# DRAM copies of weight strips and residual tiles laid out in eight row groups with gaps

## The chip, the cores and the metric

The kernel runs on one core of one Trainium2 chip. The metric is the device time in microseconds (us) of one execution. The kernel before took 2142.14 us (median of 3 runs, 2141.03 to 2143.61).

Engine names in the profile: PE is TensorE's matrix multiplication, PEld its weight loads, DVE VectorE, ACT ScalarE, POOL GpSimd, SP SyncE, which issues nearly all DMA here (its queue q1 has 152,016 of the 158,307 packets). A trailing q (SPq) means the engine's sequencer. q1 is SyncE's DMA queue; q8 is a queue that fetches instructions.

## The reference

Four residual blocks in a row, layers A, B, A, B, on a sequence of 2048 rows of 576 values:

```python
x = x + _A_ref(_layernorm(x), A_wqkv, A_wo)
x = x + _B_ref(_layernorm(x), B_mem0, B_Wq, B_Wk, B_Wv, B_Wo, B_seg_len)
x = x + _A_ref(_layernorm(x), A_wqkv, A_wo)
x = x + _B_ref(_layernorm(x), B_mem0, B_Wq, B_Wk, B_Wv, B_Wo, B_seg_len)
```

`_A_ref` projects to q, k, v with a 576 x 1728 matrix, does a local attention over 8 positions with a step of 2, and projects back with a 576 x 576 matrix. `_B_ref` is an attention over 64 segments of 32 rows, one after the other, with 32 heads of 128 and a memory of 8 rows carried along. B's weights stay in SBUF. A's weights are not kept beside them: they lie in DRAM as twelve "strips" and are fetched again for each of the 32 tiles of 64 rows in both A layers.

## The kernel before

The DRAM copies, the ring of SBUF tiles that receives the strips, and the functions that fill them (cuts marked with `# ...`):

```python
dp = self.pool("dram", 1, space=bass.MemoryType.DRAM)
self.x1T = dp.tile([P, NT, 5, T], F32, name="x1T")           # residual tiles, P = 128
self.x3T = dp.tile([P, NT, 5, T], F32, name="x3T")
self.strips = [dp.tile([P, 5 * 256], BF16, name=f"strip{i}") for i in range(12)]
# ...
tiles("ring", 3, [P, 5 * 256])                               # three tiles in SBUF
# ...
def wload(self, i, src, rows, col0, n, prio, dep):
    # ...
    w = pl.buf("ring") if k else None
    # ...
    def fetch(e):
        dma(out=w.t[:, 0:5 * n], in_=self.strips[i][:, 0:5 * n])      # n = 256 or 128
    # ...
    o = pl.op("SP", 0.9 if k <= COPY else 0.5, gather if k <= COPY else fetch, prio,
              [dep, self.strip_in.get(i)], acq=[w], lat=4.0)
    if k == COPY:
        self.strip_in[i] = pl.op("SP", 0.5, lambda e: dma(out=self.strips[i][:, 0:5 * n], in_=w.t[:, 0:5 * n]), prio, [o], uses=[w])
    return view, (w,), o
```

The first three uses of a strip gather it from the input (`COPY` is 2), the third also stores it compactly; later uses call `fetch`. The kernel plans the order of all instructions itself before it emits them: `pl.op` takes an estimated duration, and `lat=4.0` tells the plan that a refill lands 4.0 us after its issue. The matmuls that use a strip:

```python
def mm(e, c=c, view=view, ps=ps, w0=w0):
    for kc in range(5):
        nc.tensor.matmul(ps.t[:, c * T:(c + 1) * T], lhsT=view()[:, kc, w0:w0 + P], rhs=xn.t[:, kc, :],
                         start=(kc == 0), stop=(kc == 4))
```

Three strips (two of 320 KB, one of 160 KB) serve one group of 25 such matmuls, and the ring has three tiles. So a tile can be refilled only when the matmuls of the group before have left it.

## Time and profile before

| what | value | how to read it |
|---|---|---|
| time | 2142.14 us | the profiled execution spans 2133.8 us |
| TensorE busy | 2017.4 us | 95% of the span, so 116 us idle in all |
| TensorE waiting for strips | 7.0 us | lines L570 (qkv) and L680 (projection) |
| TensorE waiting for instructions ("issue") | 32.6 us | 66 waits |
| mean granted clock of TensorE | 0.987 | 1 is full speed |

The lines behind these are in the prediction. For the strips, this line of the kernel before has the issues by SyncE, with shortest, median and longest duration in ns, and first and last start in us:

```profile
L507 SPq DMA_DIRECT2D ring<-strip x732: 319/382/2679, 134.7 to 2048.2; - x183
```

The 732 refills are 244 groups of three. SyncE needs 0.38 us to issue one.

### The profile page before, as it was taken

How to read it: one execution, taken by the hardware profiler on the slowest of the kernel's cores; microseconds unless marked ns; L12 is line 12 of the kernel's file. 1: busy time of each engine (PE TensorE's matmuls, PEld its weight loads, DVE VectorE, ACT ScalarE, POOL GpSimd, SP SyncE). 2: the span in 40 equal slices, each digit the busy share in tenths (PEclk: the TensorE clock that was granted, in tenths of full speed). 3: DMA queues.
4: the chain of work that ended last, by engine and by line, in shares of the span. 5: the costliest groups of instructions: out<-in, count | busy, mean ns of one | idle time of the engine just before them, and what ended most of it. 6: DMA issues, size and time to landing. Idle time of an engine off the chain costs nothing.

```text
span 2133.8 us, 132983 instructions
## 1 busy us (share of the span) xinstructions
PE 2017.4 (95%) x60717; PEld 1732.3 (81%) x60717; DVE 1416.8 (66%) x3754; ACT 1137.8 (53%) x2803; POOL 832.5 (39%) x1289
## 2 busy tenths in 40 slices
PE   1688999999999999999999999999999999999998
PEld 1577888888888888888888888888888888888876
DVE  4477676766666666766766676667667666665565
ACT  1354555555555555555555555555555555655554
POOL 3235434444343344434444443343444334342320
PEclk7899999999999999999999999999999999999999
DMA  9744343343443344334333433334344333331220
GB/s 324 201 148 141 122 127 123 124 138 106 126 127 121 113 124 141 113 117 127 126 116 117 142 121 119 116 127 127 118 128 130 115 117 124 123 121 59 75 76 10
DMA packets 158307, 265.14 MB, mean 124 GB/s; under 512 B 23464, under 2 KB 89904, under 8 KB 157616
## 3 DMA queue, kind: packets, MB, share of 16 engines
q1 hardware_dynamic: 152016, 237.38, 35.5%
q0 software_dynamic: 4576, 18.88, 2.6%
q8 instruction: 474, 7.77, 1.5%
q14 instruction: 89, 0.73, 0.1%
q10 hardware_dynamic: 1152, 0.39, 0.1%
HBM read 240.46 MB, written 16.12 MB: 120 GB/s over the span
## 4 chain that ended last, share of the span: by engine, by line
PE 89%; DMA 6%; issue 2%; DVE 2%; ACT 1%; SPq 0%; ACTq 0%; DVEq 0%
PE r L832 29%; PE r L994 18%; PE r L879 17%; PE r L570 7%; PE r L835 7%; DMA ring<-strip 3%; PE r L970 3%; PE r L680 2%; PE r L644 2%; PE r L470 2%; PE r L929 1%; PE r L919 1%; DMA x<-in_B_mem_dram 1%; PE r L619 1%; PE r L923 1%
## 5 line engine op out<-in xcount | busy, mean ns | idle before, releaser
L832 PE MATMUL r<-hT,wq 128*128 128x80 bf16 (+1 forms) x8832 | 660.3, 198 | 4.6 <-ACT hT L276 2.8
L832 PE MATMUL r<-hT,wk 128*128 128x80 bf16 (+1 forms) x8832 | 662.5, 199 | 1.5 <-issue 1.3
L832 PEld LDWEIGHTS <-wq 128*128 128x128 bf16 x8832 | 500.9, 99 | 47.7 <-issue 35.0
L835 PE MATMUL r<-hT,wqk_r 128*128 128x160 bf16 (+1 forms) x2208 | 507.1, 230 | 0.2 <-issue 0.2
L276 ACT ACTIVATE qk<-r 128x480 bf16<-128x480 f32 (+2 forms) x668 | 351.0, 526 | 265.7 <-PE r L835 254.7
L832 PEld LDWEIGHTS <-wk 128*128 128x128 bf16 x8832 | 447.1, 99 | 1.5 <-issue 1.4
L994 PE MATMUL r<-OT,wo 128*128 128x80 bf16 (+1 forms) x11040 | 418.6, 200 | 27.6 <-issue 22.9
L994 PEld LDWEIGHTS <-wo 128*128 128x128 bf16 x11040 | 394.8, 100 | 39.4 <-issue 34.5
L879 PE MATMUL r<-wv,hT 128*32 128x512 bf16 x5376 | 355.5, 381 | 2.4 <-issue 2.0
L283 POOL TENSOR_TENSOR big<-qT,kT 128x1024 bf16<-128x1024 bf16 x189 | 314.7, 1685 | 60.3 <-ACT kT L276 33.7
L283 POOL TENSOR_TENSOR ex<-ex,sum 128x320 bf16<-128x320 bf16 x138 | 106.9, 775 | 570.7 <-DVE sum L779 509.2
L879 PEld LDWEIGHTS <-hT 128*32 128x32 bf16 x6720 | 173.1, 96 | 127.8 <-issue 5.0
L276 ACT ACTIVATE V<-r 128x512 bf16<-128x512 f32 x305 | 181.4, 596 | 159.2 <-PE r L879 159.1
L835 PEld LDWEIGHTS <-wqk_r 128*128 128x128 bf16 x2208 | 219.7, 99 | 0.5 <-issue 0.4
L768 DVE TENSOR_REDUCE nmx<-r 128x8 f32<-128x320 f32 x276 | 133.3, 483 | 108.6 <-PE r L923 108.4
L276 ACT ACTIVATE OT<-r 128x320 bf16<-128x320 f32 (+1 forms) x378 | 134.4, 423 | 112.3 <-PE r L970 111.7
L570 PE MATMUL r<-xn,ring 128*128 128x64 bf16 x4725 | 176.9, 194 | 15.6 <-DMA ring<-in_A_wqkv_dram 11.6
L570 PEld LDWEIGHTS <-ring 128*128 128x128 bf16 x4725 | 157.4, 98 | 34.5 <-issue 14.1
L276 ACT ACTIVATE big<-r 128x256 bf16<-128x256 f32 (+1 forms) x288 | 109.1, 430 | 89.4 <-PE r L644 88.4
L283 POOL TENSOR_TENSOR xnb<-x,st 128x256 bf16<-128x256 f32 x124 | 64.6, 521 | 205.4 <-DVE st L476 205.4
L1013 DVE CAST hT<-r 128x64 bf16<-128x64 f32 (+1 forms) x68 | 14.9, 219 | 194.9 <-PE r L994 194.8
L769 DVE TENSOR_TENSOR r<-r,nmx 128x320 f32<-128x320 f32 x276 | 137.8, 499 | 9.5
(147 smaller groups left out, 2978.6 us busy)
## 6 DMA issues: line engine op xcount, KB each, us to landing
ring<-strip SPq DMA_DIRECT2D x488, 320.0 KB, 3.5
ring<-strip SPq DMA_DIRECT2D x244, 160.0 KB, 4.0
x1T<-x SPq DMA_DIRECT2D x32, 160.0 KB, 3.9
x<-x1T SPq DMA_DIRECT2D x32, 160.0 KB, 4.1
x3T<-x SPq DMA_DIRECT2D x32, 160.0 KB, 4.5
x<-x3T SPq DMA_DIRECT2D x32, 160.0 KB, 4.5
wo<-in_B_Wo_dram POOLq DMA_DIRECT2D x4, 1152.0 KB, 26.0
wq<-in_B_Wq_dram POOLq DMA_DIRECT2D x2, 2048.0 KB, 20.6
```

The lines of the kernel that those rows point to most:

```text
L276: nc.scalar.activation(out=out, in_=in_, func=ACT.Copy, scale=1.0 if scale is None else scale)
L283: (self.nc.vector if e == "DVE" else self.nc.gpsimd).tensor_tensor(out=out, in0=in0, in1=in1, op=op)
L470: nc.tensor.matmul(psf, lhsT=(self.ones if c < 4 else self.ones_h)[:, :], rhs=xs.t[:, c].rearrange("p a t -> p (a t)"), start=(c == 0), st ...
L570: nc.tensor.matmul(ps.t[:, c * T:(c + 1) * T], lhsT=view()[:, kc, w0:w0 + P], rhs=xn.t[:, kc, :], start=(kc == 0), stop=(kc == 4))
L644: nc.tensor.matmul(ps[g].t[:, c * P:(c + 1) * P], lhsT=self.epadT[q4, c0 + c, :], rhs=e_.t[q4].rearrange("p w t -> p (w t)"), start=True, ...
L768: nc.vector.tensor_reduce(out=m, in_=v, axis=AX.X, op=ALU.max, negate=True)
L769: nc.vector.tensor_tensor(out=v, in0=v, in1=m.unsqueeze(len(shp) - 1).to_broadcast(shp), op=ALU.add)
L832: nc.tensor.matmul(pv[:, hh, wi, a:b], lhsT=self.Wb[wi][0][:, kc, h * P:(h + 1) * P], rhs=hT.t[:, kc, a:b], start=(hh == 0 and wi == 0 and ...
L835: nc.tensor.matmul(pv[:, hh, :, a:b], lhsT=self.Wb[0][1][:, h * P:(h + 1) * P], rhs=hT.t[:, 4:6, a:b], start=False, stop=(hh == n - 1), sk ...
L879: nc.tensor.matmul(ps.t[c * 32:(c + 1) * 32, :], lhsT=l, rhs=w, start=(kc == 0), stop=(kc == 4))
L970: nc.tensor.matmul(ps[c].t[:, i * n + a - c0:i * n + z - c0], lhsT=V[b].t[q4, r, i, :], rhs=pt.t[q4, i, b, a:z], start=(i == 0 and b == bl ...
L994: nc.tensor.matmul(psY.t[:, mb * W80 + c0:mb * W80 + c1], lhsT=self.wo[:, w0:w0 + P], rhs=self.OT[:, h % 16 // 4 * 8 + h // 16 * 4 + h % 4 ...
```

## The change

Its intent, as far as the diff tells: to give the transfers of strips and residual tiles a slowest dimension of 8 on the DRAM side. A row group of 16 rows is followed by one unused row, so 8 x 16 rows can't be read as 128 rows with one stride.

```diff
+NQU = 8
+RQU = P // NQU
-        self.x1T = dp.tile([P, NT, 5, T], F32, name="x1T")
-        self.x3T = dp.tile([P, NT, 5, T], F32, name="x3T")
-        self.strips = [dp.tile([P, 5 * 256], BF16, name=f"strip{i}") for i in range(12)]
+        self.x1T = dp.tile([NQU, P // NQU + 1, NT, 5, T], F32, name="x1T")
+        self.x3T = dp.tile([NQU, P // NQU + 1, NT, 5, T], F32, name="x3T")
+        self.strips = [dp.tile([NQU, P // NQU + 1, 5 * 256], BF16, name=f"strip{i}") for i in range(12)]
@@ fetch
-            dma(out=w.t[:, 0:5 * n], in_=self.strips[i][:, 0:5 * n])
+            dma(out=w.t[:, 0:5 * n], in_=self.strips[i][:, 0:RQU, 0:5 * n])
@@ the strip's store, likewise [:, 0:RQU, 0:5 * n]; the residual tiles' store and load:
-  out=(self.x1T if layer == 1 else self.x3T)[:, j], in_=xT.t[:]
+  out=(self.x1T if layer == 1 else self.x3T)[:, 0:RQU, j], in_=xT.t[:]
-  out=b.t[:], in_=src[:, j]
+  out=b.t[:], in_=src[:, 0:RQU, j]
```

The two added lines of constants move the line numbers behind them by two: L570 before is L572 after. The plan is not told anything new, so the order of all instructions is the same.

More of the change, by code (lines that the diff above doesn't have):

```diff
@@ L512, in wload @@
         if k == COPY:
-            self.strip_in[i] = pl.op("SP", 0.5, lambda e: dma(out=self.strips[i][:, 0:5 * n], in_=w.t[:, 0:5 * n]), prio, [o], uses=[w])
+            self.strip_in[i] = pl.op("SP", 0.5, lambda e: dma(out=self.strips[i][:, 0:RQU, 0:5 * n], in_=w.t[:, 0:5 * n]), prio, [o], uses=[w])
         return view, (w,), o
@@ L688, in a_tile @@
                   pr(Q[6]), [o], uses=[ps, xT])
-        xst = pl.op("SP", 0.5, lambda e: nc.sync.dma_start(out=(self.x1T if layer == 1 else self.x3T)[:, j], in_=xT.t[:]),
+        xst = pl.op("SP", 0.5, lambda e: nc.sync.dma_start(out=(self.x1T if layer == 1 else self.x3T)[:, 0:RQU, j], in_=xT.t[:]),
                     pr(0.95), [o], uses=[xT])
@@ L714, in residual @@
         src = (self.x1T, self.x3T)[lane]
-        o = pl.op("SP", 0.5, lambda e: nc.sync.dma_start(out=b.t[:], in_=src[:, j]), prio,
+        o = pl.op("SP", 0.5, lambda e: nc.sync.dma_start(out=b.t[:], in_=src[:, 0:RQU, j]), prio,
                   [dep, (self.x1_stored, self.x3_stored)[lane][j]], acq=[b] if xb is None else [b, xb])
```

## The prediction

Two words of the text: k is the number of completion packets that a transfer leaves on q1. In the trace of the kernel before it is 8 for the one transfer with 8 rows and 16 for those with 128; I took it for the number of DMA engines that the transfer uses. A page is what one q8 packet carries: 16,384 bytes, 474 packets, about one per 256 instructions of TensorE. That k would fall to 8, and that the eight engines would be those of the 8-row load, was my assumption; the trace of the kernel before does not show it.

> **What bounds the kernel now.** I read the page first, then the waits of the matrix engine, the list of DMA issues and the records of single packets. From the page, in order: span, engines, DMA queues, the chain that ended last, DMA issues.
>
> ```profile
> span 2133.8 us, 132983 instructions
> PE 2017.4 (95%) x60717; PEld 1732.3 (81%) x60717; DVE 1416.8 (66%) x3754; ACT 1137.8 (53%) x2803; POOL 832.5 (39%) x1289
> ...
> q1 hardware_dynamic: 152016, 237.38, 35.5%
> ...
> q8 instruction: 474, 7.77, 1.5%
> ...
> PE 89%; DMA 6%; issue 2%; DVE 2%; ACT 1%; SPq 0%; ACTq 0%; DVEq 0%
> ...
> ring<-strip SPq DMA_DIRECT2D x488, 320.0 KB, 3.5
> ring<-strip SPq DMA_DIRECT2D x244, 160.0 KB, 4.0
> x1T<-x SPq DMA_DIRECT2D x32, 160.0 KB, 3.9
> ```
>
> TensorE is busy 95% of the span and 89% of the chain. SyncE's DMA queue (q1) takes 35.5% of sixteen engines; 732 of its transfers refill the three ring tiles with weight strips. q8 fetches instructions: 474 packets, one per 256 of TensorE's 121,500 instructions. The table of time stretches shows how full TensorE is between start and end (length, then busy time of PE, PEld, DVE, ACT, POOL, then granted clock, DMA share, GB/s):
>
> ```profile
> 300.00:700.00 400.00, 394.72 (x11759) 342.49 (x11755) 273.20 (x718) 222.02 (x538) 166.37 (x260) 1.00 0.39 122
> ```
>
> So a transfer matters only through TensorE's idle time. TensorE's waits (total us, times, longest):
>
> ```profile
> PE r L994 <- issue: 22.9, 34, 1.3
> ...
> PE r L680 <- DMA ring<-strip: 3.6, 9, 0.9
> PE r L570 <- DMA ring<-strip: 3.4, 6, 1.1
> ```
>
> Only 7.0 us go to late strips. The largest wait, "issue", is the instruction stream: of 66 issue waits of PE (32.6 us), 80% ended 1.25 to 1.53 us after a q8 packet had finished. All waits of PE sum to 36 us between 135 and 1900 us, so nothing can make this kernel 2% faster by waits of DMA alone.
>
> **How late a strip may be.** Each group of 25 matmuls (qkv part, or output projection) uses three strips: two of 320 KB, one of 160 KB. There are 244 such groups. SyncE issues a refill some 0.03 us after the first tile is free, the second 0.41 us and the third 0.90 us later (medians). From a strip's own issue to its first matmul, the third strip has 4.5 us at the tenth percentile, 4.9 at the quarter, 5.6 at the median; the second 4.7, 5.1, 5.9; the first 4.5 or more in 95%. The third lands 4.0 us after its issue (median). The room is thus small: about 1.6 us at the median, under 0.85 us in a quarter of the groups.
>
> [...] the one transfer with 8 rows (the load of the initial memory) left 8 data packets of 1152 bytes and 8 completion packets; the 128-row ones leave 16 completions. [...] q1's data packets in flight peak at 16, but at 15 while an instruction packet is in flight. [...] The trace has 474 packets of 16,384 bytes, mean 1.07 us each, and shows they are not wholly hidden (32.6 us above).
>
> **The change, part by part.** The programs hold the same instructions in the same order on all engines. What differs is 872 transfers: 732 refills, 12 strip stores, 128 stores and loads of residual tiles. Their DRAM side becomes 8 x 16 rows with a gap of one row, so it can't be merged to 128; SBUF's side stays 128. [...] Bytes and rows stay.
>
> *Packets.* Eight completions fewer per transfer: q1 should show 152,016 - 872 x 8 = 145,040.
>
> *Moving time.* A row of 2560 bytes takes an engine 102 ns (median), a row of 1280 bytes 55 ns. Eight rows per engine were 0.82 us (0.44 for the small strip); sixteen are 1.63 us (0.88). A set of three moves in 4.14 us instead of 2.07.
>
> *Landing.* I took 19 sets of three with no other SyncE transfer near, times from the first issue: first packet 0.96 us, last completion of the first strip 2.46, of the second 3.29, of the third 4.93 (medians), landing 0.4 after. The third varies from 3.7 to 5.3 us. With 0.42 us of moving after the second, 3.7 is what sixteen even engines give; the extra 1.2 us is about one 16 KiB packet, so I read it as one engine held up by an instruction fetch.
>
> *Which engine is that?* I followed each engine's packets (the next usually starts 3 to 4 ns before the last one ends) through the saturated start, from 26 us to the first instruction packet at 38.2 us. Its engine is not one of the eight that carried the 8-row load. If so, after the change the strips run on eight engines that TensorE's instruction packets do not use: half the engines, but no straggler, and an instruction fetch without strips in its way. This is the step I trust least; I give it 0.85.
>
> *Cost on the strips.* Strip 1 completes at 2.46 + 0.82 = 3.28, strip 2 at 3.28 + 1.63 = 4.91, strip 3 at 4.91 + 0.88 = 5.79 us after the first issue; plus 0.42 to land. From their own issues: 3.7, 4.9, 5.3 us, against 3.0, 4.05, 4.0 (medians) before. Set against the room in each of the 244 groups, and giving a third strip issued late credit for its lateness, 87 groups come short by 40 us together (mean 0.46). A wait inside a group helps the next one: its first tile is free and being refilled while TensorE still waits for the third. I take half off: 20 us, less the 7 us that exist: +13. The 7 us also contain straggler hits that vanish.
>
> *SyncE's issue.* An issue of the 128-row form takes 0.38 us, of the 64-row loads 0.48 (medians); I allow 0.1 us more per changed issue. The engines' queue is the limit then, so only the first strip sees it. About +4 us.
>
> *Instruction fetch.* From the point where TensorE passes half a page to the start of the fetch, 1.8 us pass when q1 is under 10% busy, and 2.6 when over 50%. Without strips there, I take half of 32.6 us off: -15. A matmul wait on a strip also gives a page time to come.
>
> *Other parts.* The 12 stores lie in the start, +2. Residual tiles (128 transfers) take about 0.5 us longer, off the path. Other engines' instruction packets may share the eight: +3.
>
> Sum: 13 + 4 - 15 + 2 + 3 = +7 on 2142; rounded up for what queues behind longer transfers: 2152.
>
> **Rivals.** *A: instruction packets share the eight engines.* For: I inferred the engine. Then the third strip is late by the full 2.07 us and the straggler stays; first-order shortfall with 0.9, 1.7 and 2.1 us added is 184 us in 157 groups, and page fetches wait longer. With relief and more "issue": 2290 to 2380. Against: the packet tracing. *B: everything hidden, or k stays 16.* For: only 7 us of strip waits now, DMA 39% busy. Against: a quarter of groups has under 0.85 us. It would make 2120 to 2145. *C: SyncE becomes the bound, if the new form is issued much slower.* 997 issues at 0.38 us are 380 us; even doubled they fit, but a third issue later than 1.5 us would add directly: 2180 to 2250. Against: the unmerged 64-row loads cost 0.48 us.
>
> **Range and chances.** The main case puts the time at 2120 to 2190; A (0.12) and C (0.08) reach far above. Range 2115 to 2250. Faster by over 2% needs 43 us, more than the issue waits hold: 0.04. Slower by over 2%: A and C, and a main case mis-sized in the relief: 0.25.
>
> **What would show it.** Right: 145,040 q1 packets; landing 4.3 us or so for 320 KB strips and 5.3 for 160 KB; waits of PE on strips 20 to 40 us in 60 to 100 waits; "issue" waits of PE halved; instruction packets near 0.9 us. Wrong: packets unchanged (k stayed 16); "issue" waits doubled, with instruction packets well over 1.07 us (A); SyncE issues near 1 us (C).

## The result

The changed kernel took 2311.47 us (median of 4 runs, 2308.09 to 2316.26), the kernel before in the same rounds 2141.59 us (4 runs, 2138.08 to 2143.61). The ratio is 1.0797, with a 95% interval of 1.0772 to 1.0821. Ratios here and below are the mean time of one kernel's runs over that of the other's of the same rounds, so not quite the ratio of the medians quoted. Executions over 1.5% slower than the fastest of the same kernel are left out of the means. The result is right in value (the output agrees with the reference). The predicted 2152 and its range up to 2250 were wrong.

The page of the changed kernel, in order: span, engines, the queues q1 and q8, and the chain that ended last, by engine and by line:

```profile
span 2306.4 us, 132983 instructions
...
PE 2068.6 (90%) x60717; PEld 1754.8 (76%) x60717; DVE 1421.1 (62%) x3754; ACT 1140.4 (49%) x2803; POOL 834.1 (36%) x1289
...
q1 hardware_dynamic: 145040, 237.35, 32.4%
...
q8 instruction: 474, 7.77, 1.4%
...
PE 59%; DMA 36%; issue 2%; DVE 1%; SPq 1%; ACT 0%; ACTq 0%; DVEq 0%
DMA ring<-strip 33%; PE r L834 19%; PE r L996 15%; PE r L881 7%; PE r L837 4%; PE r L572 4%; PE r L682 2%; PE r L972 2%; PE r L646 1%; DMA x<-in_B_mem_dram 1%; PE r L931 1%; PE r L472 1%; PE r L921 1%; DMA ring<-in_A_wqkv_dram 1%; PE r L621 1%
```

The instruction count is the same. q1 has exactly the predicted 145,040 packets: each changed transfer leaves eight completions instead of sixteen (872 x 8 = 6976 packets fewer), and I take it to go out on eight engines. The counts of packets in flight agree: after 300 us, with no instruction packet in flight, the commonest number of q1's data packets above zero is eight (36% of the time). In the kernel before it is sixteen (12%), and fifteen (8%) while an instruction packet is in flight. TensorE's share of the chain fell from 89% to 59%, and the refills now carry a third of it.

TensorE's waits (total us, times, longest us), with "issue" of the output projection for comparison:

```profile
PE r L572 <- DMA ring<-strip: 83.9, 158, 2.8
PE r L682 <- DMA ring<-strip: 31.2, 33, 1.8
PE r L996 <- issue: 21.8, 25, 3.1
```

Late strips cost 115.1 us in 191 waits instead of 7.0 in 15; 76 us of it, in 88 waits, stand before the eleventh matmul of a group, the first that uses the second wide strip. Over all lines, "issue" waits came to 41.6 us instead of 32.6 (here and below these are counted from 0.05 us up, strip waits from 0.15 us as in the lists of waits).

The span grew by 172.6 us. All waits of TensorE together went from 112.0 to 233.3 us (+121), and its busy time from 2017.4 to 2068.6 us (+51); the two sum to the whole. Of the +121, strips are 108 and issue 9. The +51 needs a closer look, because the work is the same. Two groups show most of it. The list of groups (count, busy us, mean ns of one, idle before), first of the kernel before:

```profile
L570 PE MATMUL r<-xn,ring 128*128 128x64 bf16 x4725 | 176.9, 194 | 15.6 <-DMA ring<-in_A_wqkv_dram 11.6 <-DMA ring<-strip 3.4 <-issue 0.2
L680 PE MATMUL r<-oT,ring 128*128 128x64 bf16 x1575 | 62.7, 193 | 3.9 <-DMA ring<-strip 3.6
```

and then of the changed one:

```profile
L572 PE MATMUL r<-xn,ring 128*128 128x64 bf16 x4725 | 207.9, 195 | 107.0 <-DMA ring<-strip 83.9 <-DMA ring<-in_A_wqkv_dram 14.2 <-issue 5.0
L682 PE MATMUL r<-oT,ring 128*128 128x64 bf16 x1575 | 66.8, 194 | 34.2 <-DMA ring<-strip 31.2 <-issue 3.0
```

One matmul takes the same 194 ns, yet the groups are busy 31.0 and 4.1 us longer. Matmuls overlap: 4725 of them at 194 ns would be 917 us, and 177 are counted. I read it so: a wait in the middle of a group breaks the overlap, and the last matmul before it is seen at full length. The 35 us over 176 additional waits are 0.2 us each, about the length of one matmul.

The rest fits the granted clock. The timeline of the changed kernel (start us, length us, engine, line, operation, count, and the wait in brackets) after one long wait:

```profile
1113.66 1.13 PE L572 MATMUL r<-xn,ring 128*128 128x64 bf16 x15 [2.47 <-DMA ring<-strip]
1114.60 0.46 PE L834 MATMUL r<-hT,wq 128*128 128x80 bf16 x4
1114.85 0.47 PE L834 MATMUL r<-hT,wk 128*128 128x80 bf16 x4
```

The same kernel in stretches of time (from:to, length, then busy time and count of PE, PEld, DVE, ACT, POOL, then granted clock, DMA share, GB/s):

```profile
300.00:700.00 400.00, 367.76 (x10770) 313.53 (x10767) 251.38 (x660) 204.51 (x495) 153.95 (x239) 1.00 0.35 113
1113.60:1116.80 3.20, 3.14 (x47) 3.02 (x48) 0.00 (x0) 0.44 (x1) 1.33 (x1) 0.52 0.36 113
1116.80:1120.00 3.20, 3.20 (x110) 2.11 (x107) 0.95 (x3) 1.60 (x3) 3.20 (x4) 1.00 0.35 126
```

After a wait of 2.47 us TensorE ran at half clock (0.5 in the clock records) until 1116.7. The counts, 47 matmuls in 3.2 us and 110 in the next, are partly of other kinds; but in the chain of this stretch eight matmuls of L834 take 0.53 us before 1116.7 and 0.29 after. The clock records hold 14 such periods (51.6 us) after the start phase, against 4 (13.8 us) in the kernel before; over the whole run the half-clock time was 109.7 us against 58.2. TensorE was busy in 72.1 us of it, against 23.4. The 48.7 us more of work at half speed are worth up to 24 us, if half clock doubles the time (the eight matmuls above took 1.8 times as long). With the 35 us above that is a little more than the 51 us, so the two overlap somewhere; their split is an estimate. The clock records of both kernels (12 before, 36 after) hold 0.5 and 1.0 only, and all but the last of each are 3.41 us long or a multiple of it.

### The profile page after: what moved, and what is told of

Same layout as the page of the kernel before. It is cut to its first block, busy times and chain, and to the rows that moved or that the text cites.

```text
span 2306.4 us, 132983 instructions
## 1 busy us (share of the span) xinstructions
PE 2068.6 (90%) x60717; PEld 1754.8 (76%) x60717; DVE 1421.1 (62%) x3754; ACT 1140.4 (49%) x2803; POOL 834.1 (36%) x1289
## 3 DMA queue, kind: packets, MB, share of 16 engines
q1 hardware_dynamic: 145040, 237.35, 32.4%
## 4 chain that ended last, share of the span: by engine, by line
PE 59%; DMA 36%; issue 2%; DVE 1%; SPq 1%; ACT 0%; ACTq 0%; DVEq 0%
DMA ring<-strip 33%; PE r L834 19%; PE r L996 15%; PE r L881 7%; PE r L837 4%; PE r L572 4%; PE r L682 2%; PE r L972 2%; PE r L646 1%; DMA x<-in_B_mem_dram 1%; PE r L931 1%; PE r L472 1%; PE r L921 1%; DMA ring<-in_A_wqkv_dram 1%; PE r L621 1%
## 5 line engine op out<-in xcount | busy, mean ns | idle before, releaser
L834 PE MATMUL r<-hT,wq 128*128 128x80 bf16 (+1 forms) x8832 | 664.4, 199 | 6.2 <-issue 2.9
L834 PE MATMUL r<-hT,wk 128*128 128x80 bf16 (+1 forms) x8832 | 665.6, 199 | 1.9 <-issue 1.9
L834 PEld LDWEIGHTS <-wq 128*128 128x128 bf16 x8832 | 504.5, 99 | 49.4 <-issue 36.9
L834 PEld LDWEIGHTS <-wk 128*128 128x128 bf16 x8832 | 449.8, 100 | 3.4 <-issue 3.3
L881 PE MATMUL r<-wv,hT 128*32 128x512 bf16 x5376 | 360.4, 385 | 1.5 <-issue 1.2
L572 PE MATMUL r<-xn,ring 128*128 128x64 bf16 x4725 | 207.9, 195 | 107.0 <-DMA ring<-strip 83.9
L572 PEld LDWEIGHTS <-ring 128*128 128x128 bf16 x4725 | 167.8, 99 | 147.7 <-DMA ring<-strip 109.1
```

Source lines behind the costliest of these rows:

```text
L834: nc.tensor.matmul(pv[:, hh, wi, a:b], lhsT=self.Wb[wi][0][:, kc, h * P:(h + 1) * P], rhs=hT.t[:, kc, a:b], start=(hh == 0 and wi == 0 and ...
L881: nc.tensor.matmul(ps.t[c * 32:(c + 1) * 32, :], lhsT=l, rhs=w, start=(kc == 0), stop=(kc == 4))
```

## The experiments

Twelve kernels ran. In the first call the kernel before took 2142.09 us, in the second 2130.64, in the third 2130.48, so compare ratios across calls. Where a text says "lone set", it means three refills with no other transfer of SyncE near, timed from the first issue, and the medians of those sets.

The questions after the result were: which of the changed transfers cost, what part belongs to the form of the transfer (gaps, slower issue) and what part to the eight engines, and through what.

### strips8 and resid8: which transfers

```diff
 # strips8: residual tiles as before
-x1T = dp.tile([NQU, P // NQU + 1, NT, 5, T]) ... [:, 0:RQU, j]
+x1T = dp.tile([P, NT, 5, T]) ... [:, j]
 # resid8: strips as before
-strips = dp.tile([NQU, P // NQU + 1, 5 * 256]) ... [:, 0:RQU, 0:5 * n]
+strips = dp.tile([P, 5 * 256]) ... [:, 0:5 * n]
```

> Only the strips in eight groups, residual tiles as before. If the strips carry the loss: 2295 to 2315 us, strip waits of PE 105 to 120 us. If residual tiles in the same queue matter: under 2270.

> Only the residual tiles in eight groups, strips as before. If the strips carry the loss: 2138 to 2155 us, strip waits 7 to 12 us. If a residual transfer on eight engines holds up the strips behind it: 2170 or more.

Measured: strips8 2316.32 us, ratio 1.0817 (1.0780 to 1.0854), with 132 us of strip waits, both a little above what was expected. resid8 2139.76 us, ratio 0.9999 (0.9957 to 1.0041), with 6.7 us of strip waits. The loss comes from the strips; grouping the residual tiles costs nothing that these runs can resolve (0.4%).

### norefill: what strip traffic costs at all

```diff
 # the kernel before; the matmuls read whatever the ring holds
 # (the rest of the call is as before)
-o = pl.op("SP", 0.9 if k <= COPY else 0.5, gather if k <= COPY else fetch, ...)
+o = pl.op("SP", 0.9 if k <= COPY else 0.5, gather if k <= COPY else None, ...)
```

> The kernel before without its 732 refills, same order (wrong result on purpose). It shows what strips cost TensorE at all. If strip traffic delays instruction fetches, as the prediction took it: issue waits of PE fall from 32.6 to about 15 us, time 2105 to 2122. Rival: the fetch is limited by itself: issue waits stay at 28 to 36 us, time 2125 to 2137 (only the 7 us of strip waits go).

Measured: 2087.71 us, ratio 0.9747 (0.9714 to 0.9779); the result is wrong (relative error 1.78). Its chain by engine:

```profile
PE 93%; DMA 3%; DVE 2%; issue 0%; ACT 0%; SPq 0%; POOL 0%; DVEq 0%; ACTq 0%
```

This is below both expectations. The waits for instructions nearly vanish with the strips (2.8 us instead of 32.6). So in the kernel before the refills cost some 54 us: 30 of it in waits for instructions, 7 in waits for strips, and 15.5 us of TensorE's busy time (2001.9 instead of 2017.4), which no run splits further.

### g16, g32, g4: a dose of the outer dimension

Each changes one number of the changed kernel, so the form with gaps stays:

```diff
-NQU = 8
+NQU = 16    # g16; 32 in g32; 4 in g4
```

> Sixteen row groups with gaps in place of eight: the transfers keep the unmerged three-dimensional form, but the outer dimension is 16. Theory 1 (half the engines): q1 packets back at 152,016, third strip lands near 5.3 to 5.7 us after the set's first issue, strip waits of PE 7 to 30 us, time 2140 to 2175 us. Theory 2 (the form itself, issued in 0.57 us instead of 0.38 and starting 0.4 us later): strip waits of 60 us or more, 2230 us or more. The start of the first packet tells whether the 0.4 us belong to the form (still 1.35 us) or to k (back near 0.96).

> The changed kernel with 32 row groups of four rows: the outer dimension is 32[...], so 152,016 packets of queue 1 again, in the same unmerged form as with 16 groups. Theory (the form costs a fixed amount and the number of completions the rest): like 16 groups, 2190 to 2220 us, issue waits of TensorE 50 to 70 us and strip waits 25 to 45 us. Rival (the number of pieces in the access pattern sets the price of issuing and starting): issue rises above 0.60 us and the time above 2235 us.

> The changed kernel with four row groups instead of eight (one number changed), so the same unmerged form and the same issue time, but a third dose of the outer dimension: 16, 8, 4. Theory (a strip lands late in proportion to the number of completions it is cut into, and TensorE waits for it where the plan left too little time): a wide strip has 32 packets on each of four engines; at the 130 to 150 ns a packet that the earlier runs show that is 4.2 to 4.8 us after the first packet at 1.35 us, so strip 1 of a lone set of three should be complete near 5.9 us after the first issue, strip 2 near 10.5, strip 3 near 12.5 (against 3.97, 5.87, 6.76 with eight). The plan asks for 244 such sets in some 2000 us, 8.2 us each, so the transfers alone become the bound: the time should be 2750 to 3200 us, with TensorE waiting for strips for over 500 us, and packets of queue 1 near 141,550. Issue by SyncE stays at 0.57 us. Rival (the loss comes from the unmerged form and the longer issue alone, with 16 against 8 giving the rest by something else than moving time): the time would stay under 2500 us.

| kernel | q1 packets | issue by SyncE, median us | first packet of a lone set, us | strips 1, 2, 3 complete, us | TensorE waits for strips, us (times) | issue waits, us | time, us | ratio (95% interval) |
|---|---|---|---|---|---|---|---|---|
| before | 152,016 | 0.38 | 0.96 | 2.46, 3.29, 4.93 | 7.0 (15) | 32.6 | 2141.59 | 1 |
| g32 | 152,016 | 0.55 | 1.30 | 2.84, 3.82, 5.14 | 14.2 (28) | 25.7 | 2136.86 | 1.0027 (1.0015 to 1.0040) |
| g16 | 152,016 | 0.54 | 1.31 | 3.02, 4.23, 5.70 | 32.8 (46) | 61.5 | 2203.96 | 1.0288 (1.0248 to 1.0327) |
| changed, 8 | 145,040 | 0.57 | 1.35 | 3.97, 5.87, 6.76 | 115.1 (191) | 41.6 | 2311.47 | 1.0797 (1.0772 to 1.0821) |
| g4 | 141,552 | 0.51 | 1.29 | 5.5, 8.7, 10.4 (8 sets) | 513.8 (356) | 0.5 | 2876.67 | 1.3502 (1.3479 to 1.3524) |

The line of the refills' issues and the waits in g32:

```profile
L509 SPq DMA_DIRECT2D ring<-strip x732: 512/552/1853, 134.0 to 2052.2; - x183
...
  PE r L572: 10.1, 18
...
  PE r L682: 4.1, 10
```

and the same line of the changed kernel:

```profile
L509 SPq DMA_DIRECT2D ring<-strip x732: 572/574/1397, 140.7 to 2222.1; - x183
```

A caution on the columns of completions: they count completion packets in order of time. By each strip's own semaphore (a recount, 26 to 40 lone sets a kernel), the three strips land at 3.00, 4.51 and 5.18 us in the kernel before, 3.19, 4.82 and 5.53 in g32, 3.84, 5.40 and 6.17 in g16, and 4.65, 6.56 and 7.33 in the changed kernel. In the kernel before the last completion of the second strip comes 0.84 us after the one before it (medians 4.51 and 3.67), and a count in order of time hides that; in the changed kernel it is 0.18 us.

g32 settles the form: gaps, a slower issue and a first packet 0.34 us later than before cost 0.3% in all. g16 fell between its two theories. When only g16 had run I read its +62 us as the price of the form. g32 refuted that, and with it my own expectation of 2190 to 2220 us. What g16 has beyond g32 is slower packets: a row of 2560 bytes took 148 ns on average, against 127 in g32 and 130 before. So its strips complete 0.2 to 0.6 us later, and its issue waits are longer too.

g4 held in time, packets and waits, but not in the packet: a row took 109 ns on average instead of the 130 to 150 expected, and the strips completed earlier than expected (5.9, 10.5, 12.5). The mean packet is thus no constant: it was 130 ns on sixteen engines (the kernel before), 129 on eight (the changed one) and 109 on four.

In g4 the chain by engine shows the last stage of this, where transfers are the bound:

```profile
DMA 66%; PE 32%; DVE 1%; issue 1%; ACT 0%; SPq 0%; ACTq 0%; DVEq 0%
DMA ring<-strip 63%; PE r L834 10%; PE r L996 8%; PE r L881 4%; PE r L572 3%; PE r L837 2%; PE r L682 2%; PE r L972 1%; DMA x<-in_B_mem_dram 1%; PE r L646 1%; DMA strip<-ring 1%; DMA ring<-in_A_wqkv_dram 1%; PE r L931 0%; DMA x1T<-x 0%; PE r L472 0%
```

The landings can be checked against the room of the prediction's tally: in each of the 244 groups of the kernel before, by how much would a strip with these landings be late. The tally gives 1 us for g32 (6 groups), 29 us for g16 (78 groups) and 158 us for the changed kernel (158 groups). Measured were 14, 33 and 115 us. With the landings by semaphore the tally gives 2, 41 and 185 us. So it puts the kernels in the right order, but its sizes are rough: it misses some waits where strips are mostly in time, and overstates where many are late. The relief that a wait gives the next group would explain the latter; no run isolates it.

### half_a and half_b: half the bytes, same form

In both kernels of the pair each refill moves the left half of each row only. Order, number and form of the transfers stay. Both results are wrong (relative error 1.33).

```diff
 # half_a, from the changed kernel; half_b does the same to the kernel before
-dma(out=w.t[:, 0:5 * n],      in_=self.strips[i][:, 0:RQU, 0:5 * n])
+dma(out=w.t[:, 0:5 * n // 2], in_=self.strips[i][:, 0:RQU, 0:5 * n // 2])
```

> The changed kernel, whose 732 refills move the left half of each row only (1280 and 640 bytes a row instead of 2560 and 1280), on purpose with a wrong result; number, form, engines in use (8) and the order of all instructions are those of the changed kernel. Theory (the loss is the moving time of a strip on half the engines, which lands later than its use): at half the bytes a lone set completes near 2.8, 3.9 and 4.8 us after the first issue, which is no later than in the kernel with 32 groups, so the waits of TensorE for strips fall from 115 us to under 15, the half-clock time after 130 us from 52 us to under 25, and the time to 2110 to 2145 us, although all transfers still go out on eight engines with the slow issue. Rival (what costs is the form with an outer dimension of 8 as such: its issue on SyncE, its late start, the use of eight engines): the time stays above 2200 us.

> The kernel before with the same halved refills, wrong on purpose: the base for the run above. Strip waits are 7 us before, so only the instruction-page waits (33 us) have something to give: 2090 to 2130 us, between the kernel before and the one without refills (0.975). Theory: the ratio of the halved pair is under 1.015 instead of 1.08.

Measured: half_a 2100.29 us, ratio 0.9869 (0.9847 to 0.9890); half_b 2088.13 us, ratio 0.9808 (0.9786 to 0.9829). So within the pair, eight engines cost 0.6% instead of 8%. Both came out below my expectations, which allowed too little for the instruction pages: issue waits fell to 4.2 and 5.8 us. The waits of half_a, which still issues each refill in 0.57 us on eight engines:

```profile
PE r L572 <- DMA ring<-strip: 6.8, 8, 2.6
...
PE r L682 <- DMA ring<-strip: 2.6, 5, 1.0
```

and its packets on q1, as many as in the changed kernel, with 137 instead of 237 MB:

```profile
q1 hardware_dynamic: 145040, 137.41, 21.5%
```

Its lone sets complete at 2.80, 3.69 and 4.40 us, no later than in g32 (by semaphore 3.26, 4.16 and 4.84 against 3.19, 4.82 and 5.53). The half-clock time after the start is 16.7 us. So neither the form, nor the use of eight engines, nor SyncE's issue costs much by itself. The loss is the time that the bytes need on eight engines, where it exceeds the room.

### g16gap: why g16's packets are slow

```diff
 # g16 with four unused rows after each group instead of one
-[16, P // NQU + 1, ...]
+[16, P // NQU + 4, ...]
```

> Sixteen row groups of eight rows, with a gap of four rows instead of one between them in DRAM, so a group starts 30,720 instead of 23,040 bytes after the last; the SBUF side and the order are those of the run with 16 groups (ratio 1.029, packets of 2560 bytes took 148 ns on average, against 127 with 32 groups). Theory D (the stride of the simultaneous rows in DRAM makes the packets slow): the packet mean changes by more than 8 ns and the time leaves 2185 to 2220 us. Theory S (sixteen rows eight partitions apart in SBUF are slow): the mean stays at 145 to 151 ns and the time at 2185 to 2220 us.

Measured: 2183.94 us, ratio 1.0262 (1.0232 to 1.0292), mean packet 144 ns. It missed both sets of bounds by a little, and it is much nearer to theory S: the DRAM stride is not what makes 16 groups slow. That it is SBUF's side is only argued; it can't be told from these runs. Nor do they show which rows move at the same time, which both theories take for granted.

### ring_a, ring_b, lat48_b: more room for the strips

More lead should cure the changed kernel and might help the kernel before. The first pair gives the third strip a tile of its own; lat48_b tells the plan of the kernel before that refills land later.

```diff
 # ring_a from the changed kernel, ring_b from the kernel before
 tiles("ring", 3, [P, 5 * 256])
+tiles("ringh", 1, [P, 5 * P])
-w = pl.buf("ring") if k else None
+w = pl.buf("ring" if n == 256 else "ringh") if k else None
 # lat48_b
-lat=4.0
+lat=4.8
```

In ring_a and ring_b the new tile is also cleared at the start, like those of the ring.

> The changed kernel, with the third (half-wide) strip of each set in a tile of its own, so that the three full tiles of the ring serve the two wide strips: the plan can issue a wide strip one tile earlier. Order of all engines changes, transfers and their form don't. Theory (the loss is lateness of strips against too short a lead, plus half clock after the long waits): waits of TensorE for strips fall from 115 us to under 25, the half-clock time from 110 us to under 75, and the time to 2150 to 2205 us, with issue waits still at 35 to 60. Rival (the grouped traffic takes throughput that no lead gives back, of the queue or of SyncE): the time stays above 2260 us.

> The kernel before, with the same additional half-wide tile for the third strip. Its strip waits are 7 us in all and its issue waits 33, so more lead has little to remove: 2115 to 2145 us by my theory; if the lead also lets the strips be spread so that instruction pages are less late, issue waits fall below 20 us and the time to 2105 to 2120 us, and this would be a version that beats both kernels. Worse than 2160 would mean that the plan's new order costs.

> The kernel before, its plan told that a refill lands 4.8 instead of 4.0 us after issue, which changes the order on all engines; transfers as before. It has 7 us of strip waits to remove and 33 us of instruction-page waits[...]. If the plan's order is as good, 2110 to 2150 us; if the larger allowance makes it order worse, as the extra tile did (ratio 1.080), over 2170 us.

Measured: ring_a 2484.79 us, ratio 1.1668 (1.1645 to 1.1690); ring_b 2299.97 us, ratio 1.0803 (1.0785 to 1.0820); lat48_b 2203.08 us, ratio 1.0336 (1.0303 to 1.0368). None came out as hoped: ring_b and lat48_b fell in the branch that their texts gave to a worse order of the plan, and ring_a in the range of its rival. The waits of ring_b show part of why its plan is worse:

```profile
PE r L971 <- DVE pt L790: 51.2, 30, 2.7
...
PE r L571 <- DMA ringh<-strip: 10.7, 10, 2.2
```

The plan reordered every engine, and TensorE now waits 51 us for a VectorE result that cost 4.7 us before; strips cost it 20 us, its busy time is 58 us longer, and half clock lasted 206 us instead of 58. So these runs say nothing about lead at a fixed order. Within the pair the eight groups still cost 1.1668 / 1.0803 = 1.080, with 126 us of strip waits in ring_a. Two larger allowances for the landing, and a fourth full tile in the ring, could not be tried: the plan found no order with 5.2 or 6.4 us, and the build refused the tile. No correct version beat the kernel before; g32, 0.3% slower, is the nearest of those with grouped strips.

## Why the prediction was wrong

**k falls from 16 to 8: right.** 145,040 packets of q1, as worked out.

**Landing: wrong, and this is the step that failed.** "Strip 1 completes at 2.46 + 0.82 = 3.28, strip 2 at 3.28 + 1.63 = 4.91, strip 3 at 4.91 + 0.88 = 5.79 us" measured 3.97, 5.87 and 6.76. Two terms were mis-sized. First, I took the median packet, 102 ns, for a sum of sixteen. The mean in the kernel before was 130 ns, because a few packets take 300 to 600 ns, and in a sum the mean counts: 16 x 130 ns = 2.08 us against the 1.63 of the text. Between strips 1 and 2 the trace has 1.90 us. Nor are the slow packets spread evenly: in the lone sets of the changed kernel each engine's first two packets took 441 and 249 ns on average, and those of the second strip 114. Second, I let the first packet stay at 0.96 us; it came at 1.35, as it did at about 1.3 in every kernel with gaps. With the mean packet and the late start, and the 0.5 us by which the first strip of the kernel before exceeds its eight mean packets (2.46 - 0.96 - 8 x 0.13 = 0.46), strip 1 would be at 1.35 + 2.08 + 0.46 = 3.89 and strip 2 at 5.97, close to what was measured; this sum was made after the result, so the closeness is a fit and no test.

**The tally of waits: rough in method, wrong in input and in the relief.** One more microsecond of lateness turns 40 us in 87 groups into 158 us in 158 groups. I then took off half for the relief that a wait gives the next group; measured against 158 it was a quarter (115). Net: +108 us where the text has +13. It is steep because the room lies close together: 0.85 us at the quarter, 1.6 at the median. g32 costs nothing, half_a hardly anything, and g4 746 us more than the kernel before beside it.

**Cost beside the waits: missing.** That a wait also raises TensorE's busy time was not in the sum: +51 us, of which 35 is broken overlap in the two strip groups and the rest fits half-clock periods.

**Instruction fetch, -15: wrong.** It went up by 9 us. The inference on the engine held, as far as counts can show: after 300 us, eight data packets of q1 are in flight for 31% of the time with an instruction packet and 36% without one, where an instruction packet on one of the eight would leave seven. The straggler went as foreseen too: the last completion of the second strip of a lone set comes 0.18 us after the one before it, not 0.84. But that does not spare the pages. From the point where TensorE passes half a page to the start of the fetch, the median is 1.39 us without refills, 1.52 in half_a and 1.55 in half_b, 2.26 in the kernel before and 2.27 in the changed one. So the delay does not need strips on the page's engine: it is as long on eight engines as on sixteen. It is not the bytes alone either: g4 moves them all, and a recount that gives 2.24 and 2.17 us for the two kernels gives it 1.65. What goes with it is how busy q1 keeps the engines: 22.9% of sixteen in g4, 21.5 and 22.6 in the halved pair, 35.5 and 32.4 in the two kernels, and 39.5 in g16, where the recount gives 2.49 us. The delay arises before the page's packet starts: the packets took 1.07 us on average in the kernel before, 1.11 in the changed one. What the strips and the pages share is not shown by any run. The text's "nothing can make this kernel 2% faster by waits of DMA alone" fell too: norefill is 2.5% faster, because refills cost busy time beside the waits.

**SyncE's issue, +4: not contradicted.** The issue rose by 0.19 us instead of 0.1; half_a over half_b (12 us) and g32 over its kernel before (0.3%, 6 us) bound what issue and late start cost together. **Other parts, +5: too high but harmless**; its +2 and +3 were guesses with no measurement behind them, and resid8 shows nothing.

**Rivals.** A's number (2290 to 2380) held the result, its mechanism did not: by the counts above the strips' packets did not give way to instruction pages, and the straggler went. That its added lateness (0.9, 1.7 and 2.1 us) is near the measured 1.65, 2.05 and 2.15 by semaphore is luck: the late first packet and the slower packets made it. The right time from a wrong cause would have been a bad lesson. B was wrong. C was wrong: the issue took 0.57 us, not near 1.

## What to carry to other kernels

Before a transfer gets fewer engines, compare its moving time, worked out with the mean and not the median packet (and a mean under the same load), with the distribution of the room before its use: here strips that landed 0.2 to 0.35 us later (g32) cost 0.3% of the time, with 14.2 us of strip waits, and 1.65 to 2.15 us later (the changed kernel), where the room is 0.85 us at the quarter and 1.6 at the median, they cost 8%, with 115.1 us in 191 waits. Count a wait of TensorE at more than its length: here 121 us more of waits came with 51 us more of busy time, of which lost overlap (35 us) and more half clock (109.7 us instead of 58.2) are my reading. And test a form and a size apart: here 32 groups kept sixteen completions a transfer at a cost of 0.3%, and half the bytes made even eight engines cheap (0.6%).

## Further measurements

- The price of the access pattern with gaps, in the four kernels with 4, 8, 16 and 32 groups: the issue on SyncE rose from 0.38 us to between 0.51 and 0.57 us, and the first packet of a lone set came 0.33 to 0.39 us later.
- The time of a packet by how the rows are grouped, at the same 152,016 packets of q1: a row of 2560 bytes took 148 ns on average with 16 groups of eight rows, 127 with 32 groups of four, and 144 with 16 groups and a larger gap in DRAM.
- "Issue" waits, which I put down to instruction pages, cost TensorE 32.6 us before, 61.5 us in g16, and 2.8 us without refills. A page's fetch started later in the kernels where q1 keeps the DMA engines busier: 1.39 us after half a page without refills, 2.27 in the changed kernel.
- The half clock of the example above began at 1113.29 us, after 3.41 us of which TensorE was idle for 2.10, and before the wait of 2.47 us was over. After the start phase (130 us) of the two kernels, the 3.41 us before a change to half clock hold at least 1.49 us of idle time (18 changes). Of the other stretches of 3.41 us at full clock, counted from the starts of the clock records, the most idle one holds 1.77 us.
